# Attention in front of two mixtures of experts: one score product for two heads, with zeros in the keys' other rows

## The chip, the core and the metric

The kernel runs on one core of a Trainium2 chip, in one launch. The time is the device time of that core in microseconds. Three runs of the kernel before gave a median of 1866.67 us (1866.61 to 1867.35). Five engines work beside each other, each through its own list of instructions in order: TensorE (PE; its loads of the stationary operand are listed apart as PEld), VectorE (DVE), ScalarE (ACT), GpSimd (POOL) and SyncE (SP), which here issues most DMAs.

## The reference

Attention over 4 sequences of 576 tokens with 8 heads of 64 channels; its output, 2304 tokens of 512 channels, goes through a mixture of 8 experts whose weights come out of eight rounds of row and column normalisation, and then through a layer of 2048 channels with a squared ReLU. Cut to what matters here:

```
scores = q @ k.T / sqrt(64)
rel = pos[:, None] - pos[None, :]
plain = (rel >= 0) & (rel < 32)                            # heads 0 to 3
dilated = (rel >= 0) & (rel < 128) & (rel % 4 == 0)        # heads 4 to 7
scores = where(mask, scores, -1e9)
attn = softmax(scores)                                     # over the keys
x = attn @ v                                               # then the two feed-forward stages
```

A query sees 32 keys at most. The tokens of heads 4 to 7 are put in an order (all residues modulo 4 one after the other) in which the dilated window is a plain one. So a block of 32 queries needs 64 keys: its own 32 and the 32 ahead of them.

## The kernel before

Attention is 24 groups: 4 sequences, 2 halves of the heads (`hg`), 3 stretches of 192 queries (`m`). One group holds 4 heads and 6 blocks of 32 queries, that is 24 pieces of 32 queries by 64 keys, and they fill one PSUM bank: 128 partitions (4 x 32 queries) by 384 columns (6 x 64 keys). Four such pieces stand under one another, in four strips of 32 partitions.

The work is a written pipeline. `slot(i)` writes, in this order, the scores of group i, the exponential and normalisation of group i-1, the products with the values of group i-4, the transposes of group i-3, some products of the next stage where `filled` says so, and the loads (`feed`). Nothing reorders this: each engine does its part of the list in the order in which it is written.

- `att_scores` (L439 on): one product with the mask (L448: `spread_q` is an identity of 32 rows that puts the mask of 32 queries into all four strips) opens the bank, and 24 products (L452) add the scores, one for each block and head. Two heads lie in the upper and lower 64 rows of one tile, so each product reads 64 rows. DVE takes the maximum of each piece (L462) and subtracts it (L463).
- `att_exp` and `att_norm`: the exponential on ACT (L467), sum and reciprocal on DVE (L472 to L474), the scaling on POOL (L475).
- `att_tr`, `att_pv`, `att_x`: transposes (L482), copies to SBUF by ACT (L487), 12 products with the values (L496), copies of the result (L528).
- `load_qk`: queries and keys of a group are one DMA on SP, 128 partitions of 3328 bytes, into a ring of three tiles; `load_v` is one DMA of 128 x 3072 bytes. In slot i the loads for the scores of slot i+2 and for the values of group i-1 are issued, the first once the scores of slot i-1 have been taken from the same buffer.
- `warm_up` (L1158): products of a tile of zeros, 512 columns wide, whose result nobody reads. Four stand behind the scores of each of slots 0, 1 and 2. Seven small ones (L1098) run ahead of everything.

Behind attention come 80 steps of the two feed-forward stages, 8221 products from 96 us on. DMAs take eight completion counters in turn, so a DMA that is issued can wait for the one eight places earlier.

Of the kernel before, what the change touches and what calls it, by code (L numbers as in the profile page):

```python
# [10 lines left out]
F32 = mybir.dt.float32  # L11
# [11 lines left out]
QB = 32  # L23
PAD = 32
KB = QB + PAD
# [3 lines left out]
QC = GB * QB  # L29
KCOLS = QC + PAD  # L30
DIL = 4
KC = DM // 128
# [19 lines left out]
def tile_kernel(ctx: ExitStack, tc: tile.TileContext, a):  # L52
# [33 lines left out]
    ident = const.tile([128, 128], F32, name="ident")  # L86
    mask = xfp.tile([128, 4 * GB + 2, KB], F32R, name="mask")
    mask_raw = xfp.tile([QB, 4 * GB + 2, KB], F32, name="mask_raw")
    spread_q = mask[:, :2].rearrange("p g k -> p (g k)")
    p_zero = [xfp.tile([128, 2, GB // 2, 4, QB], F32, name=f"pts{k}") for k in range(2)]  # L90
    wg = xfp.tile([128, KC, 32], F32, name="wg")
# [330 lines left out]

    def load_qk(i):
        if i < NG:
            b, hg, m = groups[i]
            z = qkv.tile([128, 2 * (QC + KCOLS)], F32, tag="qk", name="qk", bufs=3)
            nc.sync.dma_start(z, a["qk"][b, hg, m])
            q_t[i], k_t[i] = (y.rearrange("p (r n) -> p r n", r=2) for y in (z[:, :2 * QC], z[:, 2 * QC:]))

    def load_v(i):  # L430
        if i < NG:
            b, hg, m = groups[i]
            v_t[i] = qkv.tile([128, GB // 2, 4 * D], F32, tag="v", name="v", bufs=4)
            nc.sync.dma_start(v_t[i], a["v"][b, hg, m])

    def round_mask(g0, g1):
        nc.scalar.copy(mask[:QB, g0:g1], mask_raw[:, g0:g1])

    def att_scores(i):  # L439
        _, hg, m = groups[i]  # L440
        qt, kt = q_t.pop(i), k_t.pop(i)
        ps = psum.tile([128, 512], F32, tag="s", name="s")[:, :GB * KB].rearrange("p (g k) -> p g k", g=GB)
        k = m + 1 if hg else 0
        if hg == 0 and m > 0:
            mk = mask[:, 4:5, :].to_broadcast([128, GB, KB])
        else:
            mk = mask[:, 2 + GB * k:2 + GB * k + GB, :]
        nc.tensor.matmul(ps, spread_q, mk, start=True, stop=False, skip_group_check=True)  # L448
# [28 lines left out]
    def att_tr(i):  # L477

        ex = e_t.pop(i).rearrange("p g k -> p (g k)")
        ps = bank("s" if i >= NG - 2 else "pt")[:, :GB * KB]  # L480
        for c in range(GB // 2):
            nc.tensor.transpose(ps[:, c * 128:(c + 1) * 128], ex[:, c * 128:(c + 1) * 128], ident)  # L482
        pt_t[i] = p_zero[i % 2]
        for half in range(2):
            keys = slice(KB * half, KB * half + KB)
            copy = nc.vector.tensor_copy if half and i >= NG - 3 else nc.scalar.copy
            copy(pt_t[i][keys, half].rearrange("p c h q -> p (c h q)"), ps[keys])  # L487

    def att_pv(i):
        vt, pt = v_t.pop(i), pt_t.pop(i)  # L490
        xt_t[i] = psum.tile([128, 512], F32, tag="xt", name="xt")[:, :2 * QC].rearrange("p (r w) -> p r w", r=2)
        halves = xt_t[i].rearrange("p r (h w) -> p r h w", h=2)
        for c in range(GB // 2):
            for head in range(4):
                pr, h = divmod(head, 2)
                nc.tensor.matmul(  # L496
                    halves[D * h:D * h + D, pr, :, c * QB:c * QB + QB],
                    vt[:, c, head * D:head * D + D],
                    pt[:, :, c, head],
                    start=True,  # L500
                    stop=True,
                )
# [576 lines left out]
    with tc.manual_schedule():  # L1079
        nc.vector.memset(warm, 0.0)  # L1080
        for eng, g in ((nc.vector, slice(0, GB + 2)), (nc.gpsimd, slice(GB + 2, None))):
            for rows in (slice(QB, 2 * QB), slice(2 * QB, 128)):
                eng.memset(mask[rows, g].bitcast(F32), 0.0)
# [10 lines left out]
        nc.sync.dma_start(mask_raw[:, GB + 2:], a["mask"][:, GB + 2:])  # L1094

# [9 lines left out]
        xr = at.tile([128, 512], F32R, name="xr", bufs=1)  # L1105
        nc.vector.tensor_copy(wr, warm)
        nc.vector.memset(xr.bitcast(F32), 0.0)
        gates = []
# [79 lines left out]
        def feed(i):  # L1188
# [5 lines left out]
            if 1 <= i < 4:  # L1194
                round_mask(GB * i + 2, GB * i + GB + 2)
            if i == 3:
# [4 lines left out]
        def slot(i):  # L1201
# [17 lines left out]
            fill(i)  # L1219
            if i < 3:  # L1220
                warm_up(4)
            feed(i)
# [287 lines left out]
def _layout(x):  # L1510
# [9 lines left out]
    def pairs(z):  # L1520
        return z.reshape(B, 2, 2, 2, S, D).transpose(0, 1, 3, 5, 2, 4)
# [4 lines left out]
    ks = np.stack([kz[..., m * QC:m * QC + KCOLS] for m in range(NM)], axis=2)  # L1526

    vp = np.concatenate([np.zeros((B, 2, 4, PAD, D), v.dtype), vo], axis=3)
    vt = np.stack([vp[:, :, :, j * QB:j * QB + KB] for j in range(NB)], axis=3)
    vt = vt.reshape(B, 2, 4, NM, 2, GB // 2, KB, D).transpose(0, 1, 3, 4, 6, 5, 2, 7)  # L1530
    vt = vt.reshape(B, 2, NM, 128, GB // 2, 4 * D)

# [12 lines left out]
    def split_at(o):  # L1545
# [3 lines left out]
    masks = [  # L1549
        z[3 * (k % 2) + k // 2]  # L1550
        for z in (
# [4 lines left out]
        )  # L1556
        for k in range(GB)
    ]
    arrays = {
        "qk": np.concatenate([z.reshape(B, 2, NM, 128, -1) for z in (qs, ks)], axis=-1),  # L1560
        "v": vt,
# [5 lines left out]
        "mask": np.concatenate(  # L1567
            [np.tile(np.eye(QB, dtype=np.float32), (1, 4)).reshape(QB, 2, KB)]
            + [np.where(m, 0.0, NEG).astype(np.float32)[:, None] for m in masks],
# [24 lines left out]
```

## Time and profile before

| | |
|---|---|
| median of three runs | 1866.67 us |
| the profiled execution: its time, its span | 1866.62 us, 1864.8 us |
| first scores, last scores (group 23) | 5.6 us, 74.6 us |
| first product of the next stage without attention beside it | 84.5 us |
| PE busy over the span | 1852.2 us, 99% |
| DVE, ACT, POOL busy | 88%, 48%, 41% |

The span runs from the first to the last instruction that the profiler saw, and the execution's time is 1.8 us more. PE's share is that of modelled durations of pipelined products, so 99% says that PE hardly ever stood still, not that it ran at its peak. The chain of waits follows the last instruction back: at each step to what released it. Attention is the first 84 us, 4.5% of the span.

### The profile page before, as it was taken

What the parts mean: (1) busy time and instruction counts of PE and PEld (TensorE: products, weight loads), DVE (VectorE), ACT (ScalarE), POOL (GpSimd) and SP (SyncE); (2) the same over time, 40 slices, a digit from 0 to 9 for tenths busy, and PEclk for the clock granted to TensorE, in tenths of its full rate; (3) what the DMA queues carried; (4) which work ended last, traced back from release to release, by engine and by line L of the source; (5) the groups of instructions that cost most, each with busy time, mean ns of one, the idle gap of its engine ahead of it and who ended that gap; (6) DMA issues with size and microseconds to landing.
All of it is one profiled execution on the core that took longest, in us unless ns stands there. A gap on an engine that the chain in (4) does not pass through costs nothing.

```text
span 1864.8 us, 28269 instructions
## 1 busy us (share of the span) xinstructions
PE 1852.2 (99%) x10209; PEld 1541.8 (83%) x10209; DVE 1648.2 (88%) x2357; ACT 902.9 (48%) x1553; POOL 760.4 (41%) x650
## 2 busy tenths in 40 slices
PE   9999999999999999999999999999999999999999
PEld 7788888888888888888888888888888888888887
DVE  7788999999999999997799999999998879875775
ACT  6752444555554544543443444444343465653454
POOL 4532656556656555553323323232222443321321
PEclk9999999999999999999999999999999999999999
DMA  8785576667666665768887787777676798889562
GB/s 294 249 332 181 213 252 242 257 243 241 231 228 245 244 231 219 254 220 343 325 320 267 288 296 278 283 274 288 246 288 250 304 355 292 284 310 387 196 255 77
DMA packets 154684, 493.28 MB, mean 265 GB/s; under 512 B 16992, under 2 KB 20720, under 8 KB 154544
## 3 DMA queue, kind: packets, MB, share of 16 engines
q1 hardware_dynamic: 154208, 491.22, 71.7%
q8 instruction: 80, 1.31, 0.3%
q14 instruction: 60, 0.49, 0.1%
q10 hardware_dynamic: 336, 0.26, 0.1%
HBM read 282.67 MB, written 208.74 MB: 264 GB/s over the span
## 4 chain that ended last, share of the span: by engine, by line
PE 93%; DVE 4%; ACT 1%; issue 1%; POOL 0%; DMA 0%; SPq 0%; ACTq 0%; POOLq 0%; DVEq 0%
PE pt L646 17%; PE mm L1013 16%; PE s L1013 14%; PE s L646 11%; PE xt L646 11%; PE mm L904 10%; PE mm L840 5%; PE xt L1013 2%; PE mm L883 2%; DVE g L736 1%; PE xt L496 1%; PE s L452 1%; DVE acc L1024 1%; PE s L904 1%; PE mm L646 0%
## 5 line engine op out<-in xcount | busy, mean ns | idle before, releaser
L736 DVE TENSOR_TENSOR g<-r,g 128x512 fp32r<-128x512 f32 x268 | 306.3, 1155 | 37.0 <-ACT g L733 35.1
L766 POOL TENSOR_TENSOR r<-mix,r 128x512 f32<-128x512 f32 x67 | 87.4, 1304 | 568.8 <-DVE mix L754 494.3
L1013 PE MATMUL s<-g,mixh 128*128 128x512 f32 x670 | 207.2, 390 | 1.1 <-ACT mm L1035 0.4
L1013 PE MATMUL mm<-g,w2h 128*128 128x512 f32 x670 | 206.5, 390 | 0.7 <-ACT s L1035 0.7
L733 ACT CAST g<-r 128x512 fp32r<-128x512 f32 x268 | 166.0, 620 | 66.4 <-PE s L1013 34.3
L1024 DVE TENSOR_TENSOR acc<-mm,acc 128x512 f32<-128x512 f32 x266 | 180.5, 681 | 1.8 <-PE mm L1013 1.8
L1024 DVE TENSOR_TENSOR acc<-s,acc 128x512 f32<-128x512 f32 x260 | 171.9, 682 | 0.1
L736 DVE TENSOR_TENSOR g<-mix,g 128x512 fp32r<-128x512 f32 x201 | 158.7, 790 | 2.9 <-ACT g L733 2.9
L733 ACT CAST g<-mix 128x512 fp32r<-128x512 f32 x201 | 124.7, 621 | 72.2 <-DVE mix L754 45.1
L1013 PEld LDWEIGHTS s<-g,mixh 128*128 128x128 f32 x670 | 125.4, 188 | 29.3 <-ACT s L1035 1.7
L1013 PEld LDWEIGHTS mm<-g,w2h 128*128 128x128 f32 x670 | 125.6, 188 | 27.3 <-ACT s L1035 1.1
L250 POOL TENSOR_TENSOR raw<-raw 128x256 f32<-128x256 f32 x36 | 37.9, 1053 | 238.2 <-DVE w2l L178 214.5
L1013 PE MATMUL mm<-g,w2l 128*128 128x512 f32 x335 | 130.4, 389 | 0.0
L805 ACT COPY s<-pt 128x512 f32<-128x512 f32 x79 | 46.5, 588 | 165.3 <-PE pt L646 165.3
L764 POOL TENSOR_TENSOR mix<-mix,r 128x512 f32<-128x512 f32 x67 | 88.5, 1320 | 87.9 <-DVE g L736 87.9
L646 PE MATMUL xt<-x_hi,sumh 128*128 128x512 f32 x316 | 123.7, 391 | 0.1
L646 PE MATMUL s<-x_hi,blkh 128*128 128x512 f32 x316 | 123.5, 391 | 0.0
L646 PE MATMUL s<-x_lo,blkh 128*128 128x512 f32 x316 | 123.2, 390 | 0.0
L646 PE MATMUL pt<-x_hi,sumh 128*128 128x512 f32 x316 | 123.1, 390 | 0.0
L646 PE MATMUL xt<-x_lo,sumh 128*128 128x512 f32 x316 | 123.1, 390 | 0.0
L646 PE MATMUL xt<-x_hi,suml 128*128 128x512 f32 x316 | 123.1, 389 | 0.0
L646 PE MATMUL s<-x_hi,blkl 128*128 128x512 f32 x316 | 123.1, 389 | 0.0
(299 smaller groups left out, 5026.0 us busy)
## 6 DMA issues: line engine op xcount, KB each, us to landing
raw<-in_w SPq DMA_DIRECT2D x62, 512.0 KB, 4.2
w_blkh<-blkh SPq DMA_DIRECT2D x40, 512.0 KB, 5.1
w_blkl<-blkl SPq DMA_DIRECT2D x40, 512.0 KB, 5.9
w_sumh<-sumh SPq DMA_DIRECT2D x40, 512.0 KB, 6.2
w_suml<-suml SPq DMA_DIRECT2D x40, 512.0 KB, 4.7
w_w2h<-w2h SPq DMA_DIRECT2D x40, 512.0 KB, 5.6
w_w2l<-w2l SPq DMA_DIRECT2D x40, 512.0 KB, 5.7
blkh<-w_blkh SPq DMA_DIRECT2D x40, 512.0 KB, 3.8
```

What stands on the lines that cost most here:

```text
L250: tt(out=r[:, 1, 1], in0=r[:, 0, 1], in1=r[:, 1, 1], op=ALU.add)
L646: nc.tensor.matmul(ps, w[:, c], z[:, x, j], start=start and k == 0, stop=stop and k == 5, skip_group_check=True)
L733: after(k, lambda: nc.scalar.copy(b[:, 0], src))
L736: lambda: nc.vector.tensor_tensor(out=b[:, 1], in0=src, in1=b[:, 0].bitcast(F32), op=ALU.subtract),
L764: after(6 if i in (TURN, first[3]) else 4, lambda: nc.gpsimd.tensor_tensor(out=r3, in0=r3, in1=r5, op=ALU.subtract))
L766: sub = lambda o, x, y: nc.gpsimd.tensor_tensor(out=o, in0=x, in1=y, op=ALU.subtract)
L805: at_once(lambda: nc.scalar.copy(made["s2"], bank_b))
L840: nc.tensor.matmul(ps, w[:, c], z[:, kc], start=k == 0, stop=k == len(terms) - 1)
L883: nc.tensor.matmul(ps, wt, g, start=n == 0, stop=n == len(terms) - 1)
L904: nc.tensor.matmul(ps, g[:, c0 * 128:c0 * 128 + 128], wt[:, fc], start=k == 0 and not seeded, stop=k == 3 * FC - 1, skip_group_check=bool( ...
L1013: nc.tensor.matmul(ps, w[wt][:, c], block[n][:, g], start=start and k == 0, stop=stop and k == 2, skip_group_check=True)
L1024: nc.vector.tensor_tensor(out=o, in0=ps, in1=o, op=ALU.add)
```

## The change

One score product now takes a pair of heads. Its stationary operand is 128 rows by 32 queries: the queries of both heads of the pair, one in the upper and one in the lower 64 rows. Its moving operand is 128 rows by 128 columns: 64 columns with the first head's keys in the upper rows and zeros in the lower ones, then 64 with zeros above and the second head's keys below. So both heads come out beside one another in one strip of 32 partitions. A group has 12 such products instead of 24.

- All queries and keys lie in one tile `kq_all` with three places. The zeros are written once, by six DVE memsets at the start; a load fills the upper 64 rows (keys, then queries) and the lower 64 rows (queries, then keys) with two DMAs of 64 partitions. For group 0 the lower half is issued by ACT.
- The strips now hold (half of the blocks, pair of heads) instead of the head, so the masks differ between two pairs of strips: the mask rows are 64 instead of 32, and three masks stand for a group instead of six. The values' layout and the products with them follow that order; their number and shape stay.
- The products of zeros: none behind slot 0, two behind slot 1, four behind slot 2.

```
+            z = kq_all[:, KQW * (i % 3):KQW * (i % 3) + 2 * (QW + KW)]
+            nc.sync.dma_start(z[:D, :KW + QW], a["kq"][b, hg, m, :D])
+            eng.dma_start(z[D:, KW:KQW], a["kq"][b, hg, m, D:])
+            k_t[i] = z.rearrange("p (h n) -> p h n", h=2)
+            q_t[i] = z[:, KW:KW + QW].rearrange("p (r n) -> p r n", r=2)
-            z = qkv.tile([128, 2 * (QC + KCOLS)], F32, tag="qk", name="qk", bufs=3)
-            nc.sync.dma_start(z, a["qk"][b, hg, m])
...
-        for g in range(GB):
-            for head in range(4):
-                pr, rows = head // 2, slice(D * (head % 2), D * (head % 2) + D)
+        for c in range(CB):
+            for quarter in range(4):
+                part, pr = divmod(quarter, 2)
+                n = QB * (CB * part + c)
                 nc.tensor.matmul(
-                    ps[QB * head:QB * head + QB, 2 * (g % 3) + g // 3, :],
-                    qt[rows, pr, g * QB:g * QB + QB],
-                    kt[rows, pr, g * QB:g * QB + KB],
+                    whole[QB * quarter:QB * quarter + QB, c],
+                    qt[:, pr, n:n + QB],
+                    kt[:, :, KCOLS * pr + n:KCOLS * pr + n + KB],
...
-        nc.scalar.dma_start(mask_raw[:, :GB + 2], a["mask"][:, :GB + 2])
-        round_mask(0, GB + 2)
+        nc.scalar.dma_start(mask_raw[:, :CB + 2], a["mask"][:, :CB + 2])
+        load_qk(0, nc.scalar)
         nc.scalar.dma_start(ident, a["ident"])
-        load_qk(0)
+        round_mask(0, CB + 2)
         load_qk(1)
...
+        for k in range(3):
+            z = kq_all[:, KQW * k:KQW * k + KQW]
+            nc.vector.memset(z[D:, :KW], 0.0)
+            nc.vector.memset(z[:D, KW + QW:], 0.0)
+            if k == 0:
+                nc.vector.tensor_copy(wr, warm)
+                nc.vector.memset(xr.bitcast(F32), 0.0)
...
-            if i < 3:
-                warm_up(4)
+            if 0 < i < 3:
+                warm_up(2 * i)
```

On PE, the start of the program before (`s` is the bank of the scores, `qk` queries and keys, `xr,wr` the tile of zeros):

```order
L448 MATMUL s<-mask 128x384
L452 MATMUL s<-qk 32x64 x24
L1158 MATMUL mm<-xr,wr 128x512 x4
L448 MATMUL s<-mask 128x384
L452 MATMUL s<-qk 32x64 x24
L1158 MATMUL mm<-xr,wr 128x512 x4
L448 MATMUL s<-mask 128x384
L452 MATMUL s<-qk 32x64 x24
```

and the same place now:

```order
L457 MATMUL s<-mask 128x384
L462 MATMUL s<-kq_all 32x128 x12
L454 MATMUL s<-mask 128x384
L462 MATMUL s<-kq_all 32x128 x12
L1172 MATMUL mm<-xr,wr 128x512 x2
L454 MATMUL s<-mask 128x384
L462 MATMUL s<-kq_all 32x128 x12
L1172 MATMUL mm<-xr,wr 128x512 x4
```

The scores of slot 1 stand right behind those of slot 0, and each group's products are half as many and twice as wide.

On SP, the first DMAs before, with the counters (`DMAHW`) and engines that each issue waits for:

```order
L427 DMA qk<-in_qk 128x832 x2
L1092 DMA raw_112<-in_w 128x1024
L427 DMA qk<-in_qk 128x832
L1094 DMA mask_raw<-in_mask 32x1152
L427 DMA qk<-in_qk 128x832 [waits DMAHW1_49,PE_49]
L434 DMA v<-in_v 128x768 [waits DMAHW0_49]
L427 DMA qk<-in_qk 128x832 [waits DMAHW2_49,PE_49]
```

and now:

```order
L432 DMA kq_all<-in_kq 64x832 x2
L433 DMA kq_all<-in_kq 64x832
L1101 DMA raw_113<-in_w1 128x1024
L432 DMA kq_all<-in_kq 64x832
L433 DMA kq_all<-in_kq 64x832 [waits DMAHW0_49]
L1103 DMA mask_raw<-in_mask 64x576 [waits DMAHW1_49]
L432 DMA kq_all<-in_kq 64x832 [waits DMAHW2_49,PE_49]
L433 DMA kq_all<-in_kq 64x832 [waits DMAHW3_49]
L441 DMA v<-in_v 128x768 [waits DMAHW4_49]
```

Where a slot had two DMAs, it has three; the lower half of the third group's queries and keys now waits for the first mask's landing.

## Rows read from the trace of the kernel before

**Rows 1.** Windows: busy time of each engine, granted PE clock, DMA share, GB/s.
```profile
14.00:44.00 30.00, 27.28 (x824) 21.74 (x824) 25.50 (x63) 23.67 (x53) 13.47 (x15) 1.00 0.93 312
44.00:73.00 29.00, 28.35 (x723) 22.26 (x721) 23.58 (x57) 23.28 (x56) 16.57 (x15) 1.00 0.84 277
...
96.40:1864.80 1768.40, 1761.73 (x8221) 1471.97 (x8221) 1573.57 (x2187) 834.92 (x1405) 712.76 (x596) 1.00 0.72 264
```

**Rows 2.** The chain of waits, first 15 us: start, duration, what.
```profile
5.62 1.44 PE s L452 x48
7.06 2.00 PE mm L1158 x4
9.06 0.32 PE s L448
9.38 1.21 PE s L452 x47
10.59 1.12 PE mm L1158 x4
...
11.88 0.80 PE s L452 x48
...
13.99 0.85 PE s L452 x48
```

**Rows 3.** Timeline of DVE: its first maximum, and those of slots 1 and 2.
```profile
7.12 0.56 DVE L462 TENSOR_REDUCE mx<-s 128x6 f32<-128x384 f32 x1 [4.04 <-PE s L452]
...
10.66 0.56 DVE L462 TENSOR_REDUCE mx<-s 128x6 f32<-128x384 f32 x1 [2.39 <-PE s L452]
...
12.75 0.56 DVE L462 TENSOR_REDUCE mx<-s 128x6 f32<-128x384 f32 x1
```

**Rows 4.** The chain of waits: pieces of the slots from 54 us on.
```profile
54.18 0.99 PE s L534 x8
...
64.49 0.81 PE s L452 x48
65.29 0.85 PE xt L496 x24
...
90.75 0.57 PE s L534 x8
```

**Rows 5.** The chain of waits: its pieces of issue up to 60 us.
```profile
17.40 0.44 issue
...
24.16 0.50 issue
...
33.43 0.42 issue
...
43.84 0.21 issue
...
52.83 0.39 issue
```

**Rows 6.** The page: instructions of each engine, and the queue that brings PE's (packets, MB, share).
```profile
PE 1852.2 (99%) x10209; PEld 1541.8 (83%) x10209; DVE 1648.2 (88%) x2357; ACT 902.9 (48%) x1553; POOL 760.4 (41%) x650
...
q8 instruction: 80, 1.31, 0.3%
```

**Rows 7.** DMA issues from 14 to 73 us: size, median us to landing.
```profile
v<-in_v SPq DMA_DIRECT2D x20, 384.0 KB, 4.7
qk<-in_qk SPq DMA_DIRECT2D x18, 416.0 KB, 4.6
raw<-in_w SPq DMA_DIRECT2D x8, 128.0 KB, 4.2
```

**Rows 8.** Windows: full loads, and the second mask's load.
```profile
5.00:7.00 2.00, 2.00 (x50) 1.50 (x50) 0.00 (x0) 0.00 (x0) 0.00 (x0) 1.00 1.04 423
7.60:8.20 0.60, 0.60 (x3) 0.50 (x2) 0.56 (x2) 0.00 (x0) 0.00 (x0) 1.00 0.67 121
```

**Rows 9.** Timeline of PE: the scores of group 23 begin.
```profile
74.59 0.59 PE L452 MATMUL s<-qk 64*32 64x64 f32 x28
```

More of the change, by code (lines that the diff above doesn't have):

```diff
@@ L30 @@
 KCOLS = QC + PAD
+CB = GB // 2
+QW = 2 * QC
+KW = 2 * KCOLS
+KQW = 2 * KW + QW
 DIL = 4
@@ L86, in tile_kernel @@
     ident = const.tile([128, 128], F32, name="ident")
[L87 to L90, printed above, removed]
+    mask = xfp.tile([128, 4 * CB + 2, 1, KB], F32R, name="mask")
+    mask_raw = xfp.tile([2 * QB, 4 * CB + 2, KB], F32, name="mask_raw")
+    spread_q = mask[:, :2].rearrange("p c h k -> p (c h k)")
+    p_zero = [xfp.tile([128, 2, CB, 4, QB], F32, name=f"pts{k}") for k in range(2)]
+    kq_all = xfp.tile([128, 3 * KQW + QW], F32, name="kq_all")
     wg = xfp.tile([128, KC, 32], F32, name="wg")
@@ L432, in load_v, with round_mask @@
             b, hg, m = groups[i]
-            v_t[i] = qkv.tile([128, GB // 2, 4 * D], F32, tag="v", name="v", bufs=4)
+            v_t[i] = qkv.tile([128, CB, 4 * D], F32, tag="v", name="v", bufs=4)
             nc.sync.dma_start(v_t[i], a["v"][b, hg, m])
-    def round_mask(g0, g1):
-        nc.scalar.copy(mask[:QB, g0:g1], mask_raw[:, g0:g1])
+    def round_mask(c0, c1):
+        nc.scalar.copy(mask[:2 * QB, c0:c1, 0], mask_raw[:, c0:c1])
     def att_scores(i):
@@ L443, in att_scores @@
         k = m + 1 if hg else 0
+        whole = ps.rearrange("p (c h) k -> p c h k", h=2)
         if hg == 0 and m > 0:
[L445 to L451 removed]
+            mk = mask[:, 3, :, :].to_broadcast([128, GB, KB])
+            nc.tensor.matmul(ps, spread_q, mk, start=True, stop=False, skip_group_check=True)
+        else:
+            mk = mask[:, 2 + CB * k:2 + CB * k + CB].to_broadcast([128, CB, 2, KB])
+            nc.tensor.matmul(whole, spread_q, mk, start=True, stop=False, skip_group_check=True)
+        for c in range(CB):
+            for quarter in range(4):
+                part, pr = divmod(quarter, 2)
+                n = QB * (CB * part + c)
                 nc.tensor.matmul(
[L453 to L455 removed]
+                    whole[QB * quarter:QB * quarter + QB, c],
+                    qt[:, pr, n:n + QB],
+                    kt[:, :, KCOLS * pr + n:KCOLS * pr + n + KB],
                     start=False,
@@ L480, in att_tr @@
         ps = bank("s" if i >= NG - 2 else "pt")[:, :GB * KB]
-        for c in range(GB // 2):
+        for c in range(CB):
             nc.tensor.transpose(ps[:, c * 128:(c + 1) * 128], ex[:, c * 128:(c + 1) * 128], ident)
@@ L491, in att_pv @@
         xt_t[i] = psum.tile([128, 512], F32, tag="xt", name="xt")[:, :2 * QC].rearrange("p (r w) -> p r w", r=2)
[L492 to L495, printed above, removed]
+        for c in range(CB):
+            for quarter in range(4):
+                part, pr = divmod(quarter, 2)
+                n = QB * (CB * part + c)
                 nc.tensor.matmul(
-                    halves[D * h:D * h + D, pr, :, c * QB:c * QB + QB],
-                    vt[:, c, head * D:head * D + D],
-                    pt[:, :, c, head],
+                    xt_t[i][D * pr:D * pr + D, :, n:n + QB],
+                    vt[:, c, quarter * D:quarter * D + D],
+                    pt[:, :, c, quarter],
                     start=True,
@@ L1080, in tile_kernel @@
         nc.vector.memset(warm, 0.0)
-        for eng, g in ((nc.vector, slice(0, GB + 2)), (nc.gpsimd, slice(GB + 2, None))):
-            for rows in (slice(QB, 2 * QB), slice(2 * QB, 128)):
-                eng.memset(mask[rows, g].bitcast(F32), 0.0)
+        for eng, c in ((nc.vector, slice(0, CB + 2)), (nc.gpsimd, slice(CB + 2, None))):
+            eng.memset(mask[2 * QB:, c].bitcast(F32), 0.0)
         for z in p_zero:
@@ L1093, in tile_kernel @@
         load_qk(2)
-        nc.sync.dma_start(mask_raw[:, GB + 2:], a["mask"][:, GB + 2:])
+        nc.sync.dma_start(mask_raw[:, CB + 2:], a["mask"][:, CB + 2:])
         ps = psum.tile([128, 512], F32, tag="s", name="s")
@@ L1194, in feed @@
             if 1 <= i < 4:
-                round_mask(GB * i + 2, GB * i + GB + 2)
+                round_mask(CB * i + 2, CB * i + CB + 2)
             if i == 3:
@@ L1520, in pairs @@
     def pairs(z):
-        return z.reshape(B, 2, 2, 2, S, D).transpose(0, 1, 3, 5, 2, 4)
+        return z.reshape(B, 2, 2, 2, S, D).transpose(0, 1, 2, 5, 3, 4)
     qs = pairs(qo).reshape(B, 2, 128, 2, NM, QC).transpose(0, 1, 4, 2, 3, 5)
@@ L1526, in _layout @@
     ks = np.stack([kz[..., m * QC:m * QC + KCOLS] for m in range(NM)], axis=2)
+    qs, ks = (z.reshape(B, 2, NM, 128, -1) for z in (qs, ks))
+    upper, lower = ((ks[:, :, :, :D], qs[:, :, :, :D]), (qs[:, :, :, D:], ks[:, :, :, D:]))
+    kq = np.concatenate([np.concatenate(z, axis=-1) for z in (upper, lower)], axis=3)
     vp = np.concatenate([np.zeros((B, 2, 4, PAD, D), v.dtype), vo], axis=3)
     vt = np.stack([vp[:, :, :, j * QB:j * QB + KB] for j in range(NB)], axis=3)
-    vt = vt.reshape(B, 2, 4, NM, 2, GB // 2, KB, D).transpose(0, 1, 3, 4, 6, 5, 2, 7)
-    vt = vt.reshape(B, 2, NM, 128, GB // 2, 4 * D)
+    vt = vt.reshape(B, 2, 2, 2, NM, 2, CB, KB, D).transpose(0, 1, 4, 2, 7, 6, 5, 3, 8)
+    vt = vt.reshape(B, 2, NM, 128, CB, 4 * D)
     def first(w, n):
@@ L1549, in _layout @@
     masks = [
-        z[3 * (k % 2) + k // 2]
+        np.concatenate([z[c], z[CB + c]])
         for z in (
@@ L1556, in _layout @@
         )
-        for k in range(GB)
+        for c in range(CB)
     ]
+    spread = np.kron(np.eye(2), np.tile(np.eye(QB), (1, 2))).astype(np.float32)
     arrays = {
-        "qk": np.concatenate([z.reshape(B, 2, NM, 128, -1) for z in (qs, ks)], axis=-1),
+        "kq": kq,
         "v": vt,
```

7 lines of the change are left out of this document (2 added, 5 removed).

## The prediction

> **What bounds the kernel now.** I read the windows first: behind 96 us PE is busy 1761.73 of 1768.40 us [rows 1]. The change touches nothing there, neither an instruction nor an address, so only the 84 us of attention can move, and what they lose or gain is passed on whole. In them PE is not so tight: 27.28 of 30 us from 14 to 44 us, 28.35 of 29 behind that, with the DMA engines at 0.93 and 0.84 of their time [rows 1]. So I looked for three things: what ends last at the start, what a slot's scores cost, and what loads can bear.
>
> At the start the chain is PE's own: scores of slot 0 for 1.44 us, four products of zeros for 2.00, mask and scores of slot 1, again four for 1.12, and so on to slot 3 at 13.99 us [rows 2]. The same scores take 1.44 us in slot 0, 1.21 in slot 1 and 0.80 in slot 2, the zeros 2.00 and then 1.12: PE ran at the lower of its two levels (1.2 against 2.4 GHz) until about 10 us, although the clock column says 1.00 in this stretch [rows 8]. DVE waits for these scores: 4.04 us ahead of its first maximum, 2.39 ahead of the second, nothing ahead of the third; from there its slot is 12.75 - 10.66 = 2.09 us [rows 3], and DVE, ACT and POOL take turns on the chain. Five pieces of the chain are "issue", 0.44 + 0.50 + 0.42 + 0.21 + 0.39 = 1.96 us, in which PE or another engine waited for nothing that the profile shows [rows 5]. From 54 us on PE's own products follow each other [rows 4].
>
> **The change part by part.** The sum starts from the profiled execution: span 1864.8 and 1.8 around it, 1866.6 us, which is the median of the three runs to 0.1.
>
> *Score products.* Before, 24 products of 64 columns take 0.81 us, after a mask product [rows 4]. The nearest rows to the new form are the gate's, which also read 128 rows and write strips of 32: four of 512 columns take 0.99 us, four of 256 take 0.57 [rows 4]. So 256 columns of four products side by side cost 0.42, and 0.15 is fixed. The new scores are three groups of four with 128 columns: 3 x 0.21 + 0.15 = 0.78 us. Had the three groups to pay the fixed part each, it would be 1.08; that is the upper bound, the lower one 0.63 without any fixed part. I take 0.78, a gain of 0.02 to 0.03 a slot, and PE is on the chain in about 12 slots: -0.3 us. The mask product keeps its 384 columns, the value products their 0.85 us. The zeros cost no time on PE: before, the same columns went by as four products side by side, two in the upper rows and two in the lower.
>
> The Trainium skill, "TensorEngine Tiling (Array Packing)", Gotcha 1, says that tiles of different rows cannot use one PSUM bank at the same time. By that rule the 24 products before, all into one bank, would take turns in pairs, and the change would halve their time. The gate's rows speak against it: 6 x 0.105 + 0.15 = 0.78 with four side by side, and 0.81 was measured in one bank [rows 4]; so nothing is to be gained from that side.
>
> *Zeros.* Four products fall behind slot 0 (2.00 us) and two of four behind slot 1 (half of 1.12, 0.56) [rows 2]. What is late next: the scores of slot 1 follow those of slot 0, at 7.06 instead of 9.06, still at the lower level: 0.32 for the mask and 1.44, so they end near 8.8 instead of 10.59 [rows 2]. DVE's second maximum comes then 1.75 us earlier than 10.66, and its 2.09 a slot carries that to slot 3 [rows 3]. Bound: -1.75 if everything behind it keeps up, 0 if the keys do not.
>
> *Memsets.* Six of 64 x 448 on DVE stand ahead of its first maximum, where it waited 4.04 us; a maximum over 384 columns takes 0.56, and six as long would be 3.4 us [rows 3]. The two that slot 0 needs come first. So that wait hides them; were they longer, the first maximum would come later by the excess. The rounding of the first mask shrinks from 512 to 320 columns, 0.1 to 0.2 us at most, and loses as much if its 64 rows land later. I count 0.
>
> *Issue gaps.* Instructions reach PE in packets of 16 KB: 1.31 MB in 80, for 2 x 10209 instructions, 64 bytes each [rows 6]. So a packet is 256 instructions, 128 passes with their weight loads. The profile counts each of these products as two passes (x48 for 24 [rows 2]) and a transpose or mask product as one, so a slot has 48 + 24 + 3 + 1 = 76 passes before and 52 now. A packet lasted 1.7 slots and lasts 2.5. The gaps stand in the middle of a run of products, where a slot is about 3 us, so I read them as PE having run a packet out before the next was there; with 1.5 times the time for each, they should go. All gone: -1.96 us [rows 5]; none: 0. I take half, -1.0, because behind the first two the chain goes to other engines.
>
> *Loads.* A slot loads 416 KB of queries and keys and 384 KB of values [rows 7], at the full rate of 423 GB/s [rows 8] 1.01 + 0.93 us; the eight pieces of weights add 2.5 us over 20 slots, 0.12. Together 2.06 us, against (74.59 - 13.99)/20 = 3.03 us a slot [rows 2, 9]. Now the keys come as two DMAs of 64 partitions. The trace has one load to a part of the partitions, the second mask's, 32 of them: while it ran, 121 GB/s at 0.67 of the engines, 181 a full share, against 423/1.04 = 407, a ratio of 2.25 [rows 8]. So bounds: 1 (the two halves and the values fill each other's gaps) and 2.25. At 1 nothing changes. At 2.25 a slot needs 2.27 + 0.93 + 0.12 = 3.32 us, 0.29 more than it has, over 20 slots +5.8 us. The window of the mask also holds small pieces of the identity's load and the queue's end, so I take 2.0: 2.02 + 0.93 + 0.12 = 3.07, just a slot's length. That is +0.04 x 20 = +0.8 us, and it eats half of the start's gain, for loads at the slot's own pace cannot follow slots that come earlier: +0.9. SP issues three DMAs a slot, and each waits for the one eight places back: the keys of a slot for keys that this slot needs anyhow. Queued behind are the values, which have three slots to land in. I count nothing there.
>
> The Trainium skill, "SBUF — State Buffer", section "Can I just issue two DMAs to hit both halves?", says no: two at once, one on each half, were only 6% faster than one, and its table gives 196 GB/s for 64 partitions where 128 reach 328. By that ratio, 1.67, a slot's loads would take about 2.75 us, an estimate, and hide; the sum would be 1863.6 us. The trace agrees in direction, and is worse [rows 8].
>
> *Sum.* -0.3 - 1.75 - 1.0 + 0.8 + 0.9 = -1.35: 1866.6 - 1.35 = 1865.3 us.
>
> **The rivals.**
>
> A. The loads keep up, and everything is kept: -0.3 - 1.75 - 1.96 = -4.0, 1862.6 us. For it: at half the price of the mask's row the DMA engines have time to spare, and from 44 us on they were at 0.84. Against it: at 0.93 from 14 to 44 us there is little room [rows 1].
>
> B. The loads bound attention, and the kernel is slower. Place: the keys' landing ahead of each score product from slot 4 on. Price: 3.32 us a slot instead of 3.03, +5.8; nothing of the start or of the gaps is kept, as PE waits for keys in both: with the 0.3 of the scores gone too, 1866.6 + 5.8 = 1872.4 us. It decides from the point where a slot's two halves cost more than 3.03 - 0.93 - 0.12 = 1.98 us, about twice their price now. For it: the ratio 2.25. Against: that row is the end of a queue, and engines that get out of step would share less.
>
> C. PE's clock rises later, because the zeros are gone that kept it at work, and it waits for keys in slot 1 or 2. Then the scores of slots 2 and 3, two masks and four zeros run at the lower level: 2 x (0.64 + 0.16) + 0.88 = 2.48 us [rows 2], 0.7 more than the start saves. With half the gaps and no further loss to the loads: 1866.6 + 0.7 - 1.0 - 0.3 = 1866.0 us. For it: before full speed came, PE had gone from scores to zeros to scores without a hole [rows 2]. Against: slots 0 and 1 now follow each other without a hole if the keys are there.
>
> **How the numbers follow.** The forecast has 0.60, A 0.16, B 0.10, C 0.14. The forecast's own range is 1863.7 to 1867.2, from the bounds of the gaps and of the start. The range over all takes in A's 1862.6 and reaches towards B as far as 2 in 10 allows: 1862.6 to 1869.2. About 0.2%, 3.7 us, is what a measurement of this kernel can tell from no change, so faster means below 1862.9, slower above 1870.4. Faster: two thirds of A and a little of the forecast, 0.13. Slower: most of B, 0.08. Within: 0.79.
>
> **What would show it.** Right: scores of a slot at 0.78 us; the second maximum near 8.9 us; the issue pieces up to 60 us gone or down to half; keys landing in 5 us and more instead of 4.6, the DMA share from 14 to 44 us at 1; the last scores between 72 and 74.6 us; the rest the same to 0.3 us. Wrong: scores of 1 us (the strips of 128 rows pay the fixed part each time); waits of PE for the keys in many slots (B); scores of 1.44 us in slot 2 or 3 (C); issue gaps as before. A change of more than 0.5 us behind 96 us would overturn the first step.

## The result, and the profile after

The kernel after takes 1876.71 us (median of 6 runs, 1874.28 to 1880.75), the kernel before on the same chip 1866.90 (6 runs, 1866.54 to 1867.36). The ratio is 1.0054, 95% interval 1.0041 to 1.0067: slower by half a per cent, about 10 us. The forecast was 1865.3 us, with a range up to 1869.2. Rival B, with a chance of 0.10, named what happened, and even its 1872.4 us was too low.

The profiled execution has a time of 1876.89 us and a span of 1875.0 us. Its windows, read as those of before, show where the 10 us lie (busy time of PE, PEld, DVE, ACT, POOL; granted PE clock, DMA share, GB/s):

```profile
14.00:44.00 30.00, 22.67 (x456) 16.77 (x456) 20.56 (x52) 19.24 (x42) 11.31 (x13) 0.98 1.04 250
44.00:73.00 29.00, 25.63 (x447) 19.26 (x446) 19.86 (x49) 19.44 (x47) 11.57 (x11) 0.94 1.00 243
...
106.80:1875.00 1768.20, 1761.54 (x8221) 1471.28 (x8221) 1573.54 (x2187) 834.76 (x1405) 712.14 (x596) 1.00 0.72 264
```

Behind attention the same 8221 products take 1761.54 us where they took 1761.73 [rows 1]. From 14 to 44 us every engine has lost work, PE from 27.28 to 22.67 us, while the DMA engines are busier than before and yet move less: 250 GB/s at a share of 1.04, where it was 312 at 0.93 [rows 1]. The second half holds the same: 243 at 1.00.

What PE waited for, up to 90 us (us in total, times, the longest):

```profile
PE s L462 <- DMA kq_all<-in_kq: 10.9, 12, 1.5
```

The scores of twelve groups waited for keys, 10.9 us together: those of slots 0 to 2, 4 to 10, 21 and 22. The DMA issues of 14 to 73 us (KB each, median us from issue to landing) say the same from the other side:

```profile
kq_all<-in_kq SPq DMA_DIRECT2D x34, 208.0 KB, 7.7
v<-in_v SPq DMA_DIRECT2D x17, 384.0 KB, 8.3
raw<-in_w SPq DMA_DIRECT2D x4, 128.0 KB, 7.3
```

Every load lands late, not only the halves: the values took 4.7 us and take 8.3, the weights 4.2 and 7.3, though these two kinds are unchanged [rows 7].

The last scores, in the timeline of PE, begin at

```profile
84.99 0.86 PE L462 MATMUL s<-kq_all 128*32 128x128 f32 x24
```

and began at 74.59 [rows 9]. That difference of 10.4 us is the loss, all but 0.2 us (the span is 10.2 longer). The start, in the timeline of PE (start, duration, idle time before and what ended it), and the granted clock beside it:

```profile
5.82 0.86 PE L462 MATMUL s<-kq_all 128*32 128x128 f32 x24 [0.76 <-DMA kq_all<-in_kq]
...
7.88 1.19 PE L462 MATMUL s<-kq_all 128*32 128x128 f32 x24 [0.82 <-DMA kq_all<-in_kq]
...
11.29 1.50 PE L462 MATMUL s<-kq_all 128*32 128x128 f32 x24 [0.75 <-DMA kq_all<-in_kq]
...
15.05 0.86 PE L462 MATMUL s<-kq_all 128*32 128x128 f32 x24
```

```profile
8.00:10.00 2.00, 2.00 (x26) 1.45 (x23) 0.85 (x2) 0.45 (x1) 0.00 (x0) 0.57 1.05 228
10.00:12.00 2.00, 1.25 (x18) 0.65 (x20) 1.09 (x4) 0.01 (x1) 0.67 (x1) 0.50 1.06 234
12.00:14.00 2.00, 2.00 (x19) 1.40 (x12) 1.10 (x3) 1.00 (x3) 0.16 (x1) 0.50 1.06 269
```

The scores of slots 0, 1 and 2 each wait for their keys, and those of slot 2 run at the lower clock level, 1.50 us, where they took 0.80 before [rows 2]. Slot 3's begin at 15.05 us instead of 13.99 [rows 2]: the start's gain is gone by then.

Not all of the loss is spread evenly. Three windows of 2 us and the chain around one hole in PE:

```profile
48.00:50.00 2.00, 0.99 (x13) 0.87 (x14) 0.06 (x1) 0.00 (x0) 0.74 (x1) 0.81 1.07 272
50.00:52.00 2.00, 2.00 (x28) 1.52 (x26) 0.00 (x0) 1.25 (x4) 0.00 (x0) 0.50 0.97 248
52.00:54.00 2.00, 2.00 (x40) 1.46 (x36) 1.53 (x3) 1.23 (x4) 0.00 (x0) 0.84 0.66 161
```

```profile
45.39 0.55 PE xt L506 x13
45.94 3.07 issue
49.01 0.76 PE xt L506 x11
...
50.92 1.44 PE s L462 x24
...
57.21 0.79 PE s L462 x24
```

In the middle of one group's products with the values PE stood for 3.07 us with nothing to wait for that the profile shows; behind it the granted clock is 0.50, the lower of its two levels, and the next scores take 1.44 us instead of 0.79. In this execution some 5 us were lost by slot 12, 3.8 more at slot 13 with that hole, 0.8 by slot 14 at the low clock, hardly anything from there to slot 22, and 1.1 at the last one (starts of the mask products against those of before). These parts aren't separate causes: while PE stood the loads went on (266 GB/s in the microsecond from 46 us), from 52 to 54 us their share fell to 0.66, and no scores waited for keys again until slot 21, by when that lead was used up. Nor is the lower clock most of the loss: two of the six executions have a mean granted clock of 0.999 and 1.000 and still take 1874.28 and 1874.45 us; the other four have 0.997 or 0.998 and take 1876.53 to 1880.75.

### The profile page after: what moved, and what is told of

It reads as the page before. It is cut to its first block, busy times and chain, and to the rows that moved or that the text cites. A ratio compares the mean times of both kernels' runs of the same rounds, so it can differ in the third digit from the quotient of the medians.

```text
span 1875.0 us, 27160 instructions
## 1 busy us (share of the span) xinstructions
PE 1852.0 (99%) x9627; PEld 1538.2 (82%) x9627; DVE 1649.9 (88%) x2362; ACT 902.5 (48%) x1553; POOL 758.3 (40%) x649
## 3 DMA queue, kind: packets, MB, share of 16 engines
q8 instruction: 76, 1.25, 0.3%
## 4 chain that ended last, share of the span: by engine, by line
PE 91%; DVE 4%; DMA 3%; ACT 1%; issue 1%; SPq 0%; POOL 0%; ACTq 0%; POOLq 0%; DVEq 0%
PE pt L656 17%; PE mm L1023 16%; PE s L1023 14%; PE s L656 11%; PE xt L656 11%; PE mm L914 10%; PE mm L850 5%; PE xt L1023 2%; PE mm L893 2%; DMA kq_all<-in_kq 2%; DVE g L746 1%; DVE acc L1034 1%; PE s L914 1%; PE xt L506 1%; DMA v<-in_v 0%
```

## The experiments

The theory: transfers into 64 partitions move fewer bytes in the same DMA time than transfers into 128, and a slot's loads now take longer than the slot. Its rivals: that there are more DMAs (one more in every slot, each with its own fixed cost and completion counter), that the new score product or the masks' new form is slower, or that the start without the zeros is worse. The kernels of one batch ran on one chip beside the kernel before, which took 1867.6 us there in the first batch, 1867.9 in the second and 1867.6 in the third.

### The kernel before with its load cut at row 64

```
-            nc.sync.dma_start(z, a["qk"][b, hg, m])
+            nc.sync.dma_start(z[:D], a["qk"][b, hg, m, :D])
+            nc.sync.dma_start(z[D:], a["qk"][b, hg, m, D:])
```

> The kernel before, with nothing but its load of queries and keys cut into two DMAs: partitions 0 to 63, then 64 to 127, both on SP. Theory H (a load to half of the partitions runs at about half the rate, so the loads bound attention): about +9 us on 1866.9, 1874 to 1878; waits of PE for the keys, DMA share at 1 with some 245 GB/s from 14 to 44 us, values landing in 8 us instead of 4.7. Theory N (it is the third DMA of a slot: issue on SP, the wait for the DMA eight places back): about +9 us as well. Theory P (the products, the missing zeros and PE's clock cost it): within 1 us of 1866.9.

Measured: 1882.03 us (4 runs, 1880.91 to 1882.54), ratio 1.007 (1.0047 to 1.0092), the slowest kernel of all, with nothing else of the change in it. PE's waits up to 90 us, and a window:

```profile
PE xt L497 <- issue: 7.4, 3, 3.7
PE s L453 <- issue: 3.6, 4, 1.6
PE s L453 <- DMA qk<-in_qk: 1.8, 4, 0.6
```

```profile
14.00:44.00 30.00, 23.13 (x668) 17.84 (x665) 20.55 (x50) 18.64 (x41) 11.30 (x13) 1.00 1.04 264
```

So the halves alone bring a loss of 14 us, more than the change's 10. It shows differently, though: 11.0 us stand under issue and only 1.8 under the keys. With 76 passes in a slot instead of 52, PE uses up a packet of instructions sooner; what ties the holes to these packets stands below, under "Issue gaps".

### The kernel before with its load cut at half of the columns

```
+            h = QC + KCOLS
+            nc.sync.dma_start(z[:, :h], a["qk"][b, hg, m, :, :h])
+            nc.sync.dma_start(z[:, h:], a["qk"][b, hg, m, :, h:])
```

> The kernel before, with its load of queries and keys cut into two DMAs of all 128 partitions, each half of the columns: as many DMAs as in the change, packets of 1664 bytes instead of 3328. Theory H: within 1.5 us of 1866.9, since all partitions are reached. Theory N: +8 to +10 us, as with the halves by partitions. Theory P: no change.

Measured: 1868.64 us (10 runs, 1866.92 to 1871.56), ratio 1.000 (0.9988 to 1.0013). The same number of DMAs, of 208 KB each, as in the kernel above; what differs is the partitions that each reaches and the bytes for one partition, 1664 instead of 3328.

```profile
14.00:44.00 30.00, 25.72 (x771) 20.52 (x771) 25.08 (x63) 23.53 (x52) 13.12 (x15) 1.00 0.91 299
```

299 GB/s at a share of 0.91: the number of DMAs is not the cause.

### The change with one load of 128 partitions that brings the zeros along

```
-            nc.sync.dma_start(z[:D, :KW + QW], a["kq"][b, hg, m, :D])
-            eng.dma_start(z[D:, KW:KQW], a["kq"][b, hg, m, D:])
+            nc.sync.dma_start(z[:, :KQW], a["kq"][b, hg, m])
...
-            nc.vector.memset(z[D:, :KW], 0.0)
-            nc.vector.memset(z[:D, KW + QW:], 0.0)
```

> The change, with queries, keys and the zeros beside them as one DMA of 128 partitions of 5120 bytes a group, 655 instead of 426 kB, and no memsets of zeros. Theory H: 655 + 393 kB at 423 GB/s are 2.5 us a slot and hide in 3.03; the time falls below the kernel before by what the start and the issue gaps give, 1862.5 to 1866. Theory N: two DMAs a slot again, the same fall. Theory P: stays near 1876.7. If bytes were the cause, the time would rise above 1876.7.

Measured: 1865.88 us (10 runs, 1865.1 to 1867.55), ratio 0.9988 (0.9978 to 0.9998). It loads 640 KB a slot where the change loads 416, and is 11 us faster than it (1.7 below the kernel before on its chip, where the change is 9.8 above).

```profile
14.00:44.00 30.00, 26.23 (x562) 19.87 (x564) 25.58 (x64) 23.93 (x54) 13.03 (x15) 1.00 1.01 405
```

```profile
PE s L461 <- DMA kq_all<-in_kq: 3.5, 3, 2.3
```

```profile
72.35 0.86 PE L461 MATMUL s<-kq_all 128*32 128x128 f32 x24
```

405 GB/s at a share of 1.01, against 250 at 1.04. The score products, the masks and the zeros' products are those of the change, so none of them is slow. The memsets are gone here as well; DVE's first maximum in the change, 6.74 us instead of 7.12, shows that they cost nothing (below). The holes under issue are small here, with the DMA engines as full as in the change: in the chain up to 60 us only two of them are above 0.2 us (0.50 and 0.22), where five made 1.96 us before [rows 5]. The last scores come 2.2 us earlier than before [rows 9]. It beats both kernels, by an interval that ends 0.02% below no difference; that is too little to call a gain for good.

### The loads by themselves

Two kernels hold only the loads of the 24 groups, in stages, and write zeros as their output: attention and all that follows is left out. The first has these stages (the tiles of a stage are all different, so nothing in it waits for a buffer):

```
whole(i)                                  # 128 partitions, 416 KB
upper(i); lower(i)                        # two halves, 208 KB each
upper(i)                                  # one half alone
whole(i); values(i)
upper(i); lower(i); values(i)
upper(i); lower(i, nc.scalar)             # the lower half issued by ACT
```

> Loads alone, all computation left out; six stages of 24 groups, one behind the other on SP: (1) 128 x 3328 bytes in one DMA; (2) upper and lower 64 partitions in turn; (3) upper 64 alone; (4) one DMA of 128 and the values; (5) upper, lower, values; (6) upper on SP and lower on ACT. Theory H: stage 1 and 4 at 400 to 425 GB/s, stage 2 and 3 near 200, stage 5 near 245 to 270, stage 6 between 200 and 250 (two queues do not put the halves side by side). Theory N: stage 2 as fast as stage 1 but for the issues, some 0.45 to 0.6 us each: 213 kB in 0.6 us is 355 GB/s.

Measured, a window in each stage (PE clock, DMA share and GB/s last):

```profile
6.00:26.00 20.00, 0.00 (x0) 0.00 (x0) 1.00 1.03 404
36.00:70.00 34.00, 0.00 (x0) 0.00 (x0) 1.00 1.04 240
80.00:98.00 18.00, 0.00 (x0) 0.00 (x0) 1.00 1.04 204
110.00:150.00 40.00, 0.00 (x0) 0.00 (x0) 1.00 1.03 404
165.00:245.00 80.00, 0.00 (x0) 0.00 (x0) 1.00 1.04 258
```

The DMA engines are busy all the time in every row. Whole loads move 404 GB/s, two halves in turn 240, one half alone 204; whole loads and values together keep 404, halves and values 258. The 240 is above the near 200 that Theory H expected. The last stage missed its aim: ACT's loads had nothing to hold them back and ran during the stage before, so that the 258 holds more halves than meant. The second kernel mends that:

```
upper(i); lower(i, nc.scalar)
upper(i); lower(i); values(i)
upper(i); values(i); lower(i)
z[i][:32]                                 # 32 partitions alone
values(i)
```

> Loads alone, all computation left out, 24 groups a stage: (1) upper 64 partitions on SP and lower 64 on ACT at the same time; (2) upper, lower, values on SP; (3) upper, values, lower; (4) 32 partitions alone; (5) values alone. The stages before gave 404 GB/s for 128 partitions, 240 for halves in turn, 204 for one half. Theory H (only what is reached of the partitions counts): (1) 200 to 250, (4) 204, (5) 404, (2) by its parts 819 kB in 1.77 + 0.97 us, 299 GB/s. Theory M (values that follow halves lose too): (2) near 245, as in the changed kernel. Order should not matter much in (3).

```profile
6.00:42.00 36.00, 0.00 (x0) 0.00 (x0) 1.00 1.04 248
50.00:116.00 66.00, 0.00 (x0) 0.00 (x0) 1.00 1.03 273
125.00:193.00 68.00, 0.00 (x0) 0.00 (x0) 1.00 1.04 264
201.00:210.00 9.00, 0.00 (x0) 0.00 (x0) 1.00 1.00 212
217.00:236.00 19.00, 0.00 (x0) 0.00 (x0) 1.00 1.03 400
```

Two issuing engines bring 248, hardly more than 240 from one. The order in the queue doesn't matter much (273 and 264). And a mixture is worse than its parts: 425,984 bytes at 240 and 393,216 at 400 GB/s take 1.77 + 0.98 = 2.76 us, which is 297 GB/s; it moves 264 to 273, between what the two theories expected. In the change itself, with the weights between, it is 250.

The packets' own records in the traces (one packet brings one partition's bytes) show where a mixture loses. A packet of values, 3072 bytes, took 124 ns on the mean beside whole loads and 125 alone, 179 and 193 beside halves, and 200 in the change from 14 to 44 us. A packet of the halves, 3328 bytes, took 227 ns in turn, 204 in both of these mixtures and 222 in the change. So what slows down in a mixture is the loads of 128 partitions, which nobody changed.

### The zeros' products by themselves

The kernel before, with the change's number of zeros' products alone:

```
-            if i < 3:
-                warm_up(4)
+            if 0 < i < 3:
+                warm_up(2 * i)
```

> The kernel before, with the change's products of zeros alone (none behind slot 0, two behind slot 1, four behind slot 2). Theory F (the forecast's step: the second maximum comes 1.75 us earlier and the following slots keep it): 1.2 to 1.8 us below the kernel before. Theory C (the clock rises later and takes it back): within 0.7 us of it, with scores of 1.4 us in slot 2 or 3. Theory K (the keys of slots 3 to 5 do not come earlier): within 0.7 us, with waits for keys.

Measured: 1866.82 us (11 runs, 1864.57 to 1869.89), ratio 0.9993 (0.9984 to 1.0002). The chain at its start:

```profile
7.65 1.45 PE s L452 x48
...
9.11 5.16 DMA qk<-in_qk
...
14.32 0.87 PE s L452 x48
```

and its last scores, in the timeline:

```profile
72.70 0.87 PE L452 MATMUL s<-qk 64*32 64x64 f32 x48
```

Slot 1 comes 1.73 us earlier than the 9.38 of before [rows 2]. Behind 9 us the chain goes over to a load of keys, that of slot 4, whose scores start at 14.32 us, and in this execution the last scores still come 1.9 us earlier than before [rows 9]. But it is the fastest of the eleven, 2.3 us below their median. The medians give less, 1.1 us (1866.82 against 1867.90), with an interval that holds no difference. So the mechanism of the zeros' part is seen in one execution with loads of 128 partitions, and its size is not shown.

And the other way round, the kernel with one load of 128 partitions, with four products of zeros behind each of slots 0, 1 and 2 again:

```
-            if 0 < i < 3:
-                warm_up(2 * i)
+            if i < 3:
+                warm_up(4)
```

> The single load of 128 partitions with the zeros in it (e3_one), but four products of zeros behind each of slots 0, 1 and 2 as before. Theory F: 1 to 1.8 us above e3_one's 1865.9. Theory K: the same as e3_one within 0.5 us, because its start waits for keys (2.3 us in slot 4) and the zeros fill time that is lost anyhow.

Measured: 1866.91 us (11 runs, 1865.53 to 1868.35), ratio 0.9993 (0.9984 to 1.0002). That is not to be told from the 0.9988 without them, which was measured on another chip. Its chain begins with the first mask,

```profile
0.75 4.54 DMA mask_raw<-in_mask
```

which took 3.50 us before. The forecast had feared that the mask of 64 rows lands later, but the rows are not the reason: in the change the same mask lands in 2.3 us, and its first product begins at 4.44 us instead of 4.93. It is late in the kernels with the single long load.

### The first weights later

The same kernel with one load of 128 partitions, where the first load of weights is issued in slot 2 instead of ahead of the third group's keys:

```
-        nc.sync.dma_start(raw1.rearrange("p b c -> p (b c)"), src_w(0, 0))
...
+            if i == 2:
+                nc.sync.dma_start(raw1.rearrange("p b c -> p (b c)"), src_w(0, 0))
```

> e3_one, with the first 512 KB of expert weights issued in slot 2 instead of ahead of the third group's keys. If the waits for keys in slots 2 and 4 (0.9 and 2.3 us) are a matter of the queue's order: 1 to 2 us below e3_one, 1864 to 1865. If the weights are then late for ACT and POOL: no gain or a loss.

Measured: 1867.77 us (11 runs, 1866.27 to 1868.68), ratio 0.9997 (0.9988 to 1.0006).

```profile
PE s L461 <- DMA kq_all<-in_kq: 2.4, 3, 1.8
```

The waits for keys shrink from the 3.5 us above to 2.4, and the time doesn't. Its granted clock shows why this execution gained nothing:

```profile
16.00:18.00 2.00, 1.81 (x38) 1.43 (x40) 0.60 (x2) 0.00 (x0) 0.83 (x1) 0.66 1.03 417
18.00:20.00 2.00, 1.95 (x20) 1.43 (x16) 1.34 (x4) 0.95 (x2) 0.45 (x1) 0.50 1.04 412
```

Behind a wait of 1.83 us for keys, the scores, value products and transposes of slot 4 take 1.13, 1.55 and 0.90 us, where with the weights in their old place, behind a wait of 2.32 us and at a clock of 1.00, they took 0.86, 0.92 and 0.55. That is 1.25 us; the last scores come 1.8 us later than there. So this run doesn't say what the order of the queue alone is worth.

### Half the dose: only the keys in two halves

```
-            nc.sync.dma_start(z[:D, :KW + QW], a["kq"][b, hg, m, :D])
-            eng.dma_start(z[D:, KW:KQW], a["kq"][b, hg, m, D:])
+            nc.sync.dma_start(z[:, KW:KW + QW], a["q"][b, hg, m])
+            nc.sync.dma_start(z[:D, :KW], a["k"][b, hg, m, :D])
+            eng.dma_start(z[D:, KW + QW:KQW], a["k"][b, hg, m, D:])
```

> The change with the queries taken out of the two halves: one load of 128 partitions brings them (192 KB), and only the keys come in two loads of 64 partitions (112 KB each), so a slot has three loads of its own on SP beside the values'. Theory (transfers into 64 partitions run at some 240 GB/s, those into 128 at some 404, and attention is slowed only where the sum of a slot's transfers is above what a slot takes without them, 3.03 us): queries 0.49, keys 0.96, values 0.97, weights 0.12 us, together 2.54 us; the loads alone showed that mixtures of the two forms move some 13 % less than the parts say, which makes it 2.87 us. Both are under 3.03 us, so the loads keep up: 1865.5 to 1868 us, last scores near 75 us, waits for keys under 5 us in all, no idle piece above 1 us put to issue, DMA share in 14 to 44 us near 0.9 to 1.0. Rival 1 (what costs is that a slot's keys come in two halves at all, or what goes with their order on the queue, whatever the bytes): 1874 to 1877 us as in the change, waits for keys 8 to 12 us. Rival 2 (a mixture with 64-partition loads moves about 245 GB/s whatever its parts are): 819 KB and the weights at 245 GB/s are 3.5 us a slot, again 1876 us or above. In between, 1869 to 1873 us, if the mixture costs more than the loads alone showed.

Measured: 1870.01 us (11 runs, 1868.78 to 1871.44), ratio 1.0013 (1.0004 to 1.0022). This lies between the theory and the first rival, at the place kept for a mixture that costs more than the loads alone showed.

```profile
14.00:44.00 30.00, 24.06 (x508) 18.27 (x505) 22.87 (x58) 21.31 (x47) 12.41 (x14) 1.00 1.00 284
```

```profile
PE s L463 <- DMA kq_all<-in_k: 7.7, 8, 1.9
```

```profile
76.92 0.85 PE L463 MATMUL s<-kq_all 128*32 128x128 f32 x22
```

A slot's 819 KB (thousands of bytes in this paragraph) and its share of the weights (8 pieces of 131 KB over 20 slots, 52 KB) make 872 KB. At 284 GB/s that is 3.07 us, just above the 3.03 of a slot before; the last scores come 2.3 us later than before, and the kernel takes 2.4 us longer. In the change 872 KB at 250 GB/s are 3.49 us, and from its slot 3 at 15.05 to the last scores at 84.99 a slot takes 69.94/20 = 3.50. With 405 GB/s, the 1101 KB of the kernel with one load are 2.72 us, and PE sets the pace again. These rates are measured in the kernels themselves: where the DMA engines never rest, bytes by rate is the slot's length over again. It shows that loads set the pace, not why the rate is what it is; by the 264 to 273 GB/s of the loads alone, a slot of the change would take 3.19 to 3.30 us, and 20 slots lose only 3 to 5.5 us.

The mean of 3.03 us hides something as well. In the kernel before, the mask products that open slots 3, 10 and 23 start at

```profile
13.65 0.34 PE L448 MATMUL s<-mask 128*128 128x384 f32 x1
...
32.22 0.42 PE L448 MATMUL s<-mask 128*128 128x384 f32 x1
...
74.22 0.44 PE L448 MATMUL s<-mask 128*128 128x384 f32 x1
```

that is 2.65 us a slot from 3 to 10 and 3.23 us from there on. Loads of 3.07 us a slot are too slow for the first stretch, by up to 7 x 0.42 = 2.9 us, and fast enough for the second. So it came: by the starts of the mask products the half dose lost 2.3 us by slot 11, and its last one comes 2.3 us late. The dose also shows in the packets of values, 171 ns on the mean from 14 to 44 us, between 122 with one load and 200 in the change. It isn't pure, for its packets of queries and keys are shorter (1536 and 1792 bytes) and a slot has one DMA more.

## Why the prediction was wrong

**Where the time would change.** Right: nothing moved behind attention, to 0.2 us. That is why the last scores tell the result here; in the experiments their shift and that of the span differ by up to 1.4 us.

**Score products.** Right in size: 0.79 us on the chain against a forecast of 0.78. But of no account, since PE waited for keys in half of the slots.

**Zeros.** Near in number at the second maximum, and partly by luck. The timeline of DVE after:

```profile
6.74 0.56 DVE L472 TENSOR_REDUCE mx<-s 128x6 f32<-128x384 f32 x1 [1.36 <-PE s L462]
...
9.12 0.56 DVE L472 TENSOR_REDUCE mx<-s 128x6 f32<-128x384 f32 x1 [1.23 <-PE s L462]
...
12.87 0.56 DVE L472 TENSOR_REDUCE mx<-s 128x6 f32<-128x384 f32 x1 [1.71 <-PE s L462]
```

The second comes at 9.12 us, where it was 10.66 and 8.9 was forecast; the third at 12.87, where it was 12.75 [rows 3]. The forecast had the scores of slots 0 and 1 at the lower level, 1.44 us each, and no wait between them. They took 0.86 and 1.19 us, and PE waited 0.82 us for the keys of slot 1; the two errors nearly cancel. The gain of 1.5 us is gone one slot later, to keys and clock. With the zeros alone the scores of slots 0 and 1 took 1.44 and 1.45 us, as forecast, and the one profiled execution kept the gain, though the medians don't settle it. So what failed is the condition that everything behind keeps up.

**Memsets.** Right: DVE's first maximum, at 6.74 us instead of 7.12, waited for PE, not for them.

**Issue gaps.** Half of 1.96 us was to go; one hole of 3.07 us came. With one load of 128 partitions the two pieces that remain make 0.72 us, so the reasoning (fewer instructions a slot, a packet lasts longer) holds as long as packets come in time. What it left out is that these packets are DMA transfers as well and can come late. The DMA queues in the microsecond from 46 us, within the hole (packets, MB, share of the engines):

```profile
q1 hardware_dynamic: 94, 0.25, 96.4%
q8 instruction: 1, 0.02, 7.9%
```

A packet for PE is under way while PE stands, among the loads; its 7.9% of 16 engines are 1.26 us. It ends at 47.43, and the hole 1.58 us later. By the packets' records that is the rule here: all 14 holes of PE above 0.4 us under issue in the first 90 us, in five kernels (before, after, rows cut, columns cut, zeros alone), end 1.2 to 1.7 us after such a packet ended. This speaks for PE having waited for instructions. Why a packet comes late stays open. Full engines alone do not do it: with one load of 128 partitions they were as full (1.01), these packets took 0.93 us in the median and no such hole opened, while beside the halves they took 1.26 us in the change and 1.22 with the rows cut. With the same 76 passes a slot, the rows cut gave 11.0 us of holes and the columns cut under 3. The packets were not tried by themselves.

**Loads.** This is the step that failed, a term of +0.8 and +0.9 us that should have been about +11.5 (the change is 9.8 us above its kernel before, the same kernel with one load of 128 partitions 1.7 below its own). The forecast took a ratio of 2.0 for the halves, added the values at the full rate, and arrived at 3.07 us a slot, just what a slot had; 3.50 was measured. The ratio was not too low: two halves in turn move 240 GB/s against 404, a ratio of 1.68, and by it the same sum would have been lower still, 2.75 us. Its bound of 2.25 came from a row that doesn't hold what the forecast read in it: of the 85 packets that start from 7.6 to 8.2 us only five are the second mask's, 23 of 73 KB, and most of the others are the identity's small pieces. Alone, 32 partitions moved 212 GB/s, a ratio of 1.9. What was wrong is that the terms were added as if each kind of load kept its own rate: the values' packets, 124 ns beside whole loads, took 179 to 193 beside halves alone and 200 in the kernel. Halves and values together moved 264 to 273 GB/s alone and 250 in the kernel, where the sum of the parts says 297. The trace of before had no such mixture, and no bound was set on it: with the ratio 2.25 as the worst case the forecast's own upper bound was 3.32 us. The sum was also held against a mean slot, 3.03 us, though the slots from 3 to 10 take 2.65; even its own 3.07 us would have cost up to 2.9 us there instead of 0.8. Behind that stands a choice that its own text didn't support, since at 3.07 against 3.03 us the forecast stood right on the point from which rival B decides, and still gave B only 0.10.

The Trainium skill, "SBUF — State Buffer", section "Can I just issue two DMAs to hit both halves?", says that two transfers, one on each half, do not add up but follow each other; the prediction used its figures, 196 against 328 GB/s, for an estimate of 2.75 us. The runs agree with the direction (248 GB/s with two issuing engines against 204 for one half alone, which is a fifth more, not the page's 6%). The page's ratio of 1.67 is one for a half alone, for which the runs give 404/204 = 1.98; that halves in turn come to 1.68 is a coincidence. What that estimate missed, like the sum, is the mixture.

**Clock.** Rival C was at work too. PE waited 0.76, 0.82 and 0.75 us for the keys of slots 0 to 2, its clock stood at 0.57 and 0.50 from 8 to 14 us, and the scores and zeros of slot 2 ran at the lower level. C's price was 0.7 us more than the start saves; slot 3's scores come 1.1 us later than before. With the zeros alone, where the keys of slots 0 to 2 were there in time, the scores took 0.87 us from slot 2 on. So the missing zeros alone did not bring the clock down. That the waits for keys did is likely but not shown: with one load of 128 partitions and the change's zeros it stayed at 1.00 behind waits of 0.94 and 2.32 us, and with the weights moved it fell behind one of 1.83. It fell once more behind the hole of 3.07 us, which cost 0.65 us on one group's scores (1.44 against 0.79).

What stays open: why loads of 128 partitions slow down beside halves; why 250 GB/s in the kernel against 264 to 273 in the loads alone; and how much of the 10 us the one hole is worth by itself, as the loads went on during it. The six runs after spread over 6.5 us, those before over 0.8, but that doesn't show that the holes differ between executions: beside the three batches of experiments the kernel before spread over 10.2, 6.6 and 6.1 us itself. Only one execution of each kernel was profiled.

## What to carry to other kernels

A load that is cut by partitions is not the same load in two pieces: where a stage's DMA engines have as little time to spare as here (a share of 0.93), sum its bytes at the rate that the whole mixture reaches, and measure that with a kernel of loads alone before the cut is made (here it gave 264 to 273 GB/s, still above the kernel's 250). Hold the sum against the shortest stretch of slots, not against their mean. Here it was cheaper to load 224 KB of zeros a slot in one transfer of 128 partitions than to leave them out with two of 64. And when a sum ends within a per cent of the point where the bottleneck changes, the rival behind that point deserves far more than one chance in ten.

## What the runs showed of the hardware

- One load of 128 partitions of 3328 bytes moved 404 GB/s, two of 64 partitions in turn 240, one half alone 204, 32 rows alone 212, at a DMA share of 1.00 to 1.04 in all; cut by columns, with as many DMAs, the kernel's time did not change (ratio 1.000, 0.9988 to 1.0013).
- The unchanged loads beside the halves slow down too: values from 4.7 to 8.3 us to landing, weights from 4.2 to 7.3; a values' packet of 3072 bytes takes 124 ns beside whole loads and 200 in the change.
- Beside half loads, holes of up to 3.7 us opened in PE for which the profile names only issue; they end 1.2 to 1.7 us after the end of a packet of instructions, and so do the shorter ones of the other kernels. With whole loads at the same share (1.01) there was none above 0.4 us.
- PE's clock can be at its lower level behind such a hole (0.50 from 50 to 52 us) and behind a wait for keys (0.50 from 18 to 20 us with the weights moved), but it need not: behind a wait of 2.32 us it stayed at 1.00.
